# Merging the window's first block by a predicated copy in the attention maxima of a one-core transformer kernel

## The chip, the cores and the metric

The kernel runs on one core of a Trainium2 chip. The metric is the device time of one execution in microseconds (us). A core has a matrix engine (TensorE, PE in the profile, with its weight loads as PEld), a vector engine (VectorE, DVE), a scalar engine (ScalarE, ACT), GpSimd (POOL) and a sync engine (SP), which here issues the DMAs. TensorE writes its results into PSUM, a small memory of eight banks; SBUF is the larger working memory.

## The reference

One sequence of 2048 positions with 576 features passes through an attention block and an MLP-mixer block, each ahead of a residual addition and each with a layer norm that a condition vector modulates. The attention has 32 heads of width 18 and a sliding causal window: query i sees keys i-255 to i.

```python
scores = jnp.einsum("bhqd,bhkd->bhqk", q, k) * (Dh ** -0.5)
mask = (idx[:, None] - idx[None, :] >= 0) & (idx[:, None] - idx[None, :] < 256)
scores = jnp.where(mask[None, None], scores, -1e9)
p = softmax(scores, axis=-1)
o = jnp.einsum("bhqk,bhkd->bhqd", p, v)
...
h = layernorm(x) * (1 + ca) + sa
x = x + ga * (attention(h) @ wo)
h = layernorm(x) * (1 + cb) + sb
x = x + gb * mixer_block(h)
```

The softmax needs, for each query and head, a maximum over the allowed scores. Any number close to it serves for stability, but here it is the exact maximum over the window.

## The kernel before

The whole program is one hand-made schedule: every piece of work is entered with a time (`at(t, f, ...)`), the entries are sorted by time, and the instructions are issued in that order. Each engine works through its own instructions strictly in this order, and so does SP's DMA queue. The times only give an order; what really sets the pace is what each engine waits for.

The stages are the QKV projection, the attention, the output projection with two layer norms, the token mixing and the channel MLP. The change lies in the attention, which runs over 32 steps n. A step treats 512 queries (group g = n // 8) of four heads, as two pairs j of two heads. Queries and keys are cut into blocks of 64. For a query block the window touches five key blocks: the oldest, of which only the keys k > q (positions inside the block) are allowed, three full ones, and its own, of which only k <= q are allowed.

For the maxima, `mx` (L436) forms the scores of two query blocks i = 2 bb + s into one PSUM tile `pm` of two banks. There are eight such units (j, bb) in a step, and they use two PSUM tiles in turn (tags m0 and m1), so a unit can only start when the reduce of the unit two before it has read its tile. Each query block takes one matrix product of 320 columns with the keys (L444), and a second product, of the identity with a constant `Mq` (L446), which adds -1e30 to the forbidden places of the oldest and of the own block, 128 columns in all. In the first group (n < 8) query blocks 0 to 3 have fewer than five key blocks, since the sequence begins there; they mask their own block alone (L448). `red` (L450) takes the maximum: for the units with five blocks, one reduce over two times 320 columns on VectorE (L456), and for the others one reduce for each query block (L460). There are 224 units of the first kind and 32 of the second.

Once the eight units of step n are reduced, `mtr` (L464) transposes the maxima on TensorE (the instruction that the profile calls `mt`), `mev` (L468) copies them on ScalarE, and `mst` (L473) writes them by two DMAs into two rows of the query tile, so that the later score products come out with the maximum already subtracted. On SP's queue the loads of the queries and keys of a later step (L419, L421) stand behind these writes. From the loaded data POOL forms `QS` (L427), which `mx` reads, and `KS` (L434), which the later products read.

Two steps later `xm` (L480) computes the scores again, transposed and with the maxima subtracted, in ten banks a step, adding the masks with `Mk` (L489); `ex` (L504) applies the exponential on ScalarE. Every second step `av` (L526) multiplies by the values, 208 small products in a row, followed by transposes (L536) and the division by the sum on VectorE (L543, L544). On TensorE the units of `mx` are interleaved with these: one unit, one or two banks of `xm`, the next unit, and so on.

From step 12 on the output projection of one tile of 128 rows is spread over every two steps, ten tiles within the attention: transposes (L590), the split into two parts on ScalarE and VectorE (L597, L599), the products of its two halves (L611), the residual additions on VectorE (L615), and two layer norms, whose statistics (L117 to L119) and normalisation (L624, L625) are VectorE's too. The first half and the transposes fall into a step that also holds an `av` block, the second half and the norms into the next.

Of the kernel before, what the change touches and what calls it, by code (L numbers as in the profile page):

```python
# [9 lines left out]
F32R = mybir.dt.float32r  # L10
BF16 = mybir.dt.bfloat16
AF = mybir.ActivationFunctionType
ALU = mybir.AluOpType
# [6 lines left out]
P = 128  # L20
# [13 lines left out]
class Kern:  # L34
# [8 lines left out]
    def setup(self, stack):  # L43
        nc, tc = self.nc, self.tc
        self.ev = []
        self.cst = stack.enter_context(tc.tile_pool(name="cst", bufs=1))
        self.dr = stack.enter_context(tc.tile_pool(name="dr", bufs=1, space=DRAM))
        self.ps = stack.enter_context(tc.tile_pool(name="psU", bufs=1, space=PSUM))
        self.pools = {}
        c = self.cst  # L50
        self.ident = c.tile([P, P], F32, name="ident")
        self.identr = c.tile([P, P], F32R, name="identr")
        self.gb = c.tile([P, D], F32, name="gb")
        self.mhalf = c.tile([P, 1], F32, name="mhalf")
        self.rowm = c.tile([P, 8], F32, name="rowm")
        self.Mq = c.tile([P, 2, 64], F32R, name="Mq")
        self.Mk = c.tile([P, 5, 64], F32R, name="Mk")
        self.md = c.tile([P, 10], F32, name="md")
        self.qd = [self.dr.tile([2, D, 512], F32, name=f"qd{g}") for g in range(4)]
        self.kd = [self.dr.tile([2, D, 768], F32, name=f"kd{g}") for g in range(4)]  # L60
        self.vd = [self.dr.tile([P, VW], F32, name=f"vd{t}") for t in range(NT)]
        self.od = [self.dr.tile([512, D], F32, name=f"od{g}") for g in range(4)]
        self.xp = [self.dr.tile([P, D], F32, name=f"xp{t}") for t in range(NT)]
        self.hbd = [self.dr.tile([P, D], F32, name=f"hbd{t}") for t in range(NT)]
        self.xnd = [self.dr.tile([P, D], F32, name=f"xnd{t}") for t in range(NT)]
        self.modd = {v: self.dr.tile([1, D], F32, name=f"modd{v}") for v in (2, 3, 4, 5)}
# [24 lines left out]
    def masks(self):  # L91
        nc = self.nc
        g = nc.gpsimd
        for M in (self.Mq, self.Mk):
            g.memset(M.bitcast(F32), 0.0)
        h = slice(0, 64)
        sel = lambda t, s, op, cm: g.affine_select(out=t, in_=t.bitcast(F32), pattern=[[s, 64]], compare_op=op, fill=NEG, base=0, channel_multiplier=cm)
        sel(self.Mq[h, 0], 1, ALU.is_gt, -1)
        sel(self.Mq[h, 1], -1, ALU.is_ge, 1)
        sel(self.Mk[h, 0], -1, ALU.is_gt, 1)  # L100
        sel(self.Mk[h, 1], 1, ALU.is_ge, -1)
        nc.vector.tensor_copy(self.Mk[h, 3:5], self.Mk[h, 0:2].bitcast(F32))
        for M in (self.Mq, self.Mk):
            nc.vector.tensor_copy(M[64:128], M[0:64].bitcast(F32))
        m = self.rowm
        v = self.ident[:, 0:108].rearrange("p (u r d) -> p u r d", u=3, r=2)
        for r in range(2):
            nc.vector.tensor_reduce(out=m[:, r:r + 1], in_=v[:, :, r, :], axis=mybir.AxisListType.XY, op=ALU.add)
        nc.vector.tensor_tensor(out=m[:, 2:4], in0=m[:, 0:2], in1=self.ident[:, 108:110], op=ALU.add)
        nc.vector.tensor_reduce(out=m[:, 4:5], in_=self.ident[:, 108:110], axis=mybir.AxisListType.X, op=ALU.add)  # L110
# [277 lines left out]
    def attention(self, t1, t2, TA, HU, LX=2.05):  # L388
        nc, at, ps = self.nc, self.at, self.ps
# [46 lines left out]
        def mx(n, j, bb):  # L436
            g = n // 8
            pm = X["pm", n, j, bb] = ps.tile([P, 2, 512], F32, tag=f"m{bb % 2}", name=f"mx{n}_{j}_{bb}")
            Q, K = X["qs", n, j], X["K"][n % 3]
            for s in range(2):  # L440
                i = 2 * bb + s
                nb = 5 if g else min(5, i + 1)
                lhs = Q[:, i].rearrange("p r q -> p (r q)")
                nc.tensor.matmul(pm[:, s, 320 - 64 * nb:320], lhs, K[:, j, 64 * (i + 5 - nb):64 * (i + 5)], start=True, stop=False)  # L444
                if nb == 5:
                    nc.tensor.matmul(pm[:, s, 0:320].rearrange("p (a b) -> p a b", b=64)[:, 0::4, :], self.identr, self.Mq, start=False, stop=True)  # L446
                else:
                    nc.tensor.matmul(pm[:, s, 256:320], self.identr, self.Mq[:, 1], start=False, stop=True)  # L448

        def red(n, j, bb):  # L450
            if ("m", n) not in X:
                X["m", n] = a1([P, 16], F32, tag="m", name=f"m{n}", bufs=2)
            m, pm = X["m", n], X["pm", n, j, bb]
            c = 8 * j + 2 * bb
            if n >= 8 or bb >= 2:
                nc.vector.tensor_reduce(out=m[:, c:c + 2], in_=pm[:, :, 0:320], axis=mybir.AxisListType.X, op=ALU.max, negate=True)  # L456
            else:
                for s in range(2):
                    w = 64 * (2 * bb + s + 1)
                    nc.vector.tensor_reduce(out=m[:, c + s:c + s + 1], in_=pm[:, s, 320 - w:320], axis=mybir.AxisListType.X, op=ALU.max, negate=True)  # L460
# [201 lines left out]
        for n in range(N):  # L662
            at(max(t1 + .5 + n * .01, tm(n - 0.8)), load, n)
            for j in range(2):
                at(max(t1 + .6, tm(n - 0.3 + 0.5 * j)), qs, n, j)
                for bb in range(4):
                    th = n + (4 * j + bb) / 8
                    at(tm(th), mx, n, j, bb)
                    at(tm(th + .06), red, n, j, bb)
                at(max(t2 + .01, tm(n + LX - 0.5 + 0.45 * j)), ks, n, j)  # L670
                for k in range(5):
                    th = n + LX + (5 * j + k) / 10
                    at(tm(th), xm, n, j, k)
                    at(tm(th + .03), ex, n, j, k)
            at(tm(n + 1.03), mtr, n)
            at(tm(n + 1.04), mev, n)
            at(tm(n + 1.13), mst, n)
        for u in range(16):
            h = 2 * u + LX + 2
# [592 lines left out]
```

## Time and profile before

| what | before |
|---|---|
| median of 3 runs | 1869.98 us (1864.36 to 1878.24) |
| the profiled execution | 1870.27 us, span 1868.5 us |
| mean granted TensorE clock | 0.971 |
| PE busy | 1731.3 us, 93% |
| DVE busy | 1094.4 us, 59% |
| ACT busy | 707.2 us, 38% |
| POOL busy | 902.3 us, 48% |
| the units of the maxima | from 231 us to 698 us |

The busy time of a group of matrix products is the time in which at least one of them was in flight; the mean duration of one holds its latency, so neighbours overlap and the mean isn't what one product costs. A wait is told with the engine and line that released it; where several things were waited for it is the one that came last by the profile's account.

### The profile page before, as it was taken

How to read it: one execution, taken by the hardware profiler on the slowest of the kernel's cores; microseconds unless marked ns; L12 is line 12 of the kernel's file. 1: busy time of each engine (PE TensorE's matmuls, PEld its weight loads, DVE VectorE, ACT ScalarE, POOL GpSimd, SP SyncE). 2: the span in 40 equal slices, each digit the busy share in tenths (PEclk: the TensorE clock that was granted, in tenths of full speed). 3: DMA queues.
4: the chain of work that ended last, by engine and by line, in shares of the span. 5: the costliest groups of instructions: out<-in, count | busy, mean ns of one | idle time of the engine just before them, and what ended most of it. 6: DMA issues, size and time to landing. Idle time of an engine off the chain costs nothing.

```text
span 1868.5 us, 33751 instructions
## 1 busy us (share of the span) xinstructions
PE 1731.3 (93%) x13496; PEld 1579.5 (85%) x13496; DVE 1094.4 (59%) x1801; ACT 707.2 (38%) x1210; POOL 902.3 (48%) x842
## 2 busy tenths in 40 slices
PE   6999989889999997898879999999979999999998
PEld 6788878788888986797868899999978999999997
DVE  3644244455656563566667666666676666666664
ACT  2222134344444444444433333333343333333331
POOL 3312264445454442346466655555553555555560
PEclk9999979899999998899989999999989999999999
DMA  4855552444544533565352211111224222222211
GB/s 146 312 180 180 165 152 85 118 117 133 156 134 141 149 101 113 192 216 168 115 167 68 60 55 54 55 55 56 60 71 141 60 60 60 60 60 60 59 43 51
DMA packets 156132, 206.72 MB, mean 111 GB/s; under 512 B 19012, under 2 KB 87620, under 8 KB 155400
## 3 DMA queue, kind: packets, MB, share of 16 engines
q1 hardware_dynamic: 155976, 204.57, 35.8%
q8 instruction: 106, 1.74, 0.4%
q14 instruction: 50, 0.41, 0.1%
HBM read 143.69 MB, written 60.56 MB: 109 GB/s over the span
## 4 chain that ended last, share of the span: by engine, by line
PE 45%; DVE 3%; POOL 3%; DMA 2%; ACT 1%; issue 1%; SPq 1%; POOLq 0%; DVEq 0%
PE d L1128 23%; PE pg L789 1%; PE w L838 1%; DVE W L986 1%; DMA wf<-in_B_w_dram 1%; PE u18P L1075 1%; PE u19P L1075 1%; PE u29P L1075 1%; PE u33P L1075 1%; PE u32P L1075 1%; PE u31P L1075 1%; PE u30P L1075 1%; PE u28P L1075 1%; PE u27P L1075 1%; PE u26P L1075 1%
## 5 line engine op out<-in xcount | busy, mean ns | idle before, releaser
L1128 PE MATMUL d<-W,G 128*128 128x288 f32 x3456 | 505.9, 297 | 11.9 <-DVE acc L1136 9.1
L1128 PEld LDWEIGHTS d<-W,G 128*128 128x128 f32 x3456 | 487.9, 189 | 33.6 <-DVE acc L1136 10.3
L1136 DVE TENSOR_TENSOR acc<-d,acc 128x576 f32<-128x576 f32 x288 | 216.7, 753 | 195.9 <-PE d L1128 193.9
L966 POOL TENSOR_TENSOR wf<-wf 128x384 f32<-128x384 f32 x140 | 146.6, 1068 | 337.9 <-DMA wf<-in_B_w_dram 299.8
L456 DVE TENSOR_REDUCE m<-mx 128x2 f32<-128x640 f32 x224 | 181.3, 817 | 159.5 <-PE mx L446 157.3
L504 ACT ACTIVATE P<-X 128x512 f32<-128x512 f32 (+4 forms) x320 | 180.4, 573 | 207.2 <-PE X L489 204.6
L444 PE MATMUL mx<-KD,QS 128*128 128x320 f32 (+4 forms) x512 | 157.6, 358 | 38.2 <-POOL QS L427 19.4
L427 POOL TENSOR_SCALAR QS<-QD,rowm 128x512 fp32r<-128x512 f32 x128 | 87.7, 698 | 145.4 <-DMA QD<-qd 60.7
L487 PE MATMUL X<-QD,KS 128*128 128x64 f32 (+2 forms) x704 | 151.2, 307 | 3.7 <-ACT P L504 3.3
L978 POOL TENSOR_TENSOR W<-wf,W 128x768 fp32r<-128x768 f32 x70 | 151.4, 2185 | 1.2 <-ACT W L972 1.2
L1105 DVE TENSOR_TENSOR G<-U,G 128x512 fp32r<-128x512 f32 x108 | 91.0, 843 | 100.3 <-ACT G L1098 100.3
L444 PEld LDWEIGHTS mx<-KD,QS 128*128 128x128 f32 x512 | 101.9, 199 | 45.8 <-POOL QS L427 24.2
L1096 ACT ACTIVATE U<-U 128x512 f32<-128x512 f32 x108 | 68.3, 632 | 177.6 <-DVE U L1081 177.6
L1096 ACT ACTIVATE C<-C 128x512 f32<-128x512 f32 x36 | 22.8, 632 | 280.7 <-DVE C L1081 280.7
L279 PE MATMUL qk<-hT,Wqk 128*128 128x512 f32 x504 | 121.0, 401 | 0.0
L279 PEld LDWEIGHTS qk<-hT,Wqk 128*128 128x128 f32 x504 | 95.9, 191 | 24.2 <-issue 0.9
L487 PEld LDWEIGHTS X<-QD,KS 128*128 128x128 f32 x704 | 106.7, 195 | 10.6 <-ACT P L504 7.5
L434 POOL TENSOR_SCALAR KS<-KD,rowm 128x768 fp32r<-128x768 f32 (+1 forms) x128 | 107.6, 853 | 0.0
L992 POOL TENSOR_TENSOR wf<-wf,gb 128x1152 f32<-128x1152 f32 x35 | 103.5, 2956 | 6.7 <-DMA wf<-in_B_w_dram 6.7
L446 PE MATMUL mx<-Mq,identr 128*128 128x128 f32 x448 | 101.3, 226 | 0.0
L1007 POOL TENSOR_TENSOR W<-wf,W 128x1152 fp32r<-128x1152 f32 x35 | 96.7, 2762 | 6.9 <-ACT W L1001 6.9
L972 ACT CAST W<-wf 128x1152 fp32r<-128x1152 f32 x70 | 90.3, 1319 | 21.6 <-DMA wf<-in_B_w_dram 10.8
(763 smaller groups left out, 3219.5 us busy)
## 6 DMA issues: line engine op xcount, KB each, us to landing
wf<-in_B_w_dram SPq DMA_DIRECT2D x35, 576.0 KB
wf<-in_B_w_dram SPq DMA_DIRECT2D x140, 128.0 KB
KD<-kd SPq DMA_DIRECT2D x72, 216.0 KB
QD<-qd SPq DMA_DIRECT2D x96, 144.0 KB
wf<-in_B_w_dram SPq DMA_DIRECT2D x140, 64.0 KB
qd<-qs SPq DMA_DIRECT2D x16, 512.0 KB
kd<-qs SPq DMA_DIRECT2D x16, 512.0 KB
vd<-Vst SPq DMA_DIRECT2D x16, 312.0 KB
```

Source lines behind the costliest of these rows:

```text
L279: nc.tensor.matmul(po, W[:, a, fs], H[:, c, :], start=(n == 0), stop=(n == 13))
L434: nc.gpsimd.tensor_scalar(t[:, b0:, r], src[:, b0:], M[:, 2 + r:3 + r], 0.0, op0=ALU.mult, op1=ALU.add)
L444: nc.tensor.matmul(pm[:, s, 320 - 64 * nb:320], lhs, K[:, j, 64 * (i + 5 - nb):64 * (i + 5)], start=True, stop=False)
L456: nc.vector.tensor_reduce(out=m[:, c:c + 2], in_=pm[:, :, 0:320], axis=mybir.AxisListType.X, op=ALU.max, negate=True)
L487: nc.tensor.matmul(px[:, c:c + q1 - q0], K[:, b + 4].rearrange("p r k -> p (r k)"), Q[:, j, q0:q1], start=(i == 0), stop=False)
L504: nc.scalar.activation(p[:, lo:], X["px", n, j, k][:, lo:], AF.Exp, scale=SCALE)
L966: nc.gpsimd.tensor_tensor(out=WF[:, o], in0=WF[:, a], in1=WF[:, b], op=ALU.subtract)
L978: eng.tensor_tensor(out=W[:, s0:s1, 3:5, :], in0=WF[:, 1 + s0:1 + s1, 0:2], in1=W[:, s0:s1, 0:2, :].bitcast(F32), op=ALU.subtract)
L992: nc.gpsimd.tensor_tensor(out=R4, in0=R4, in1=gb.unsqueeze(1).to_broadcast([P, 2, D]), op=ALU.mult)
L1075: nc.tensor.matmul(po, W[:, w - 1, a, :], X[:, b, :], start=(m == 0), stop=(m == 6))
L1128: nc.tensor.matmul(po, G[:, g, ta, b, ts], W[:, w, b, cs], start=(n == 0), stop=(n == 5))
L1136: nc.vector.tensor_tensor(out=a, in0=po, in1=a, op=ALU.add)
```

## The change

The constant `Mq` keeps only its second half: -1e30 where k > q, 0 elsewhere. For query blocks with all five key blocks no mask product is issued any more; the product with the keys ends the accumulation. In `red`, VectorE first copies the scores of the oldest block over those of the own block wherever `Mq` isn't zero (read as integers, its -1e30 is a nonzero number), that is, wherever k > q. These are just the places that are forbidden in the own block and allowed in the oldest one. The maximum is then taken over the last four blocks, 256 columns for each query block instead of 320. Blocks at the beginning of the sequence keep the mask product of 64 columns and their reduces.

```diff
-        self.Mq = c.tile([P, 2, 64], F32R, name="Mq")
+        self.Mq = c.tile([P, 64], F32R, name="Mq")
...
-        sel(self.Mq[h, 0], 1, ALU.is_gt, -1)
-        sel(self.Mq[h, 1], -1, ALU.is_ge, 1)
+        sel(self.Mq[h], -1, ALU.is_ge, 1)
...
-                nc.tensor.matmul(pm[:, s, 320 - 64 * nb:320], lhs, K[:, j, 64 * (i + 5 - nb):64 * (i + 5)], start=True, stop=False)
-                if nb == 5:
-                    nc.tensor.matmul(pm[:, s, 0:320].rearrange("p (a b) -> p a b", b=64)[:, 0::4, :], self.identr, self.Mq, start=False, stop=True)
-                else:
-                    nc.tensor.matmul(pm[:, s, 256:320], self.identr, self.Mq[:, 1], start=False, stop=True)
+                nc.tensor.matmul(pm[:, s, 320 - 64 * nb:320], lhs, K[:, j, 64 * (i + 5 - nb):64 * (i + 5)], start=True, stop=nb == 5)
+                if nb < 5:
+                    nc.tensor.matmul(pm[:, s, 256:320], self.identr, self.Mq, start=False, stop=True)
...
             if n >= 8 or bb >= 2:
-                nc.vector.tensor_reduce(out=m[:, c:c + 2], in_=pm[:, :, 0:320], axis=mybir.AxisListType.X, op=ALU.max, negate=True)
+                late = self.Mq.bitcast(mybir.dt.int32).unsqueeze(1).to_broadcast([P, 2, 64])
+                nc.vector.copy_predicated(pm[:, :, 256:320], late, pm[:, :, 0:64])
+                nc.vector.tensor_reduce(out=m[:, c:c + 2], in_=pm[:, :, 64:320], axis=mybir.AxisListType.X, op=ALU.max, negate=True)
```

## The prediction

> **What bounds the kernel now.** I read the windows of busy time first, to find which engine each stretch of the attention hangs on, then the timelines of TensorE (PE) and VectorE (DVE) inside one step, then the waits. Columns of the windows: stretch, its length, busy us of PE, PEld, DVE, ACT and POOL with instruction counts, granted TensorE clock, DMA share, GB/s.
>
> ```profile
> 332.98:348.19 15.21, 15.05 (x214) 12.47 (x212) 7.81 (x13) 6.02 (x13) 8.06 (x13) 0.82 0.35 95
> 637.22:654.94 17.72, 17.30 (x303) 16.29 (x303) 8.97 (x16) 8.19 (x16) 9.23 (x12) 1.00 0.40 115
> 654.94:667.55 12.61, 11.11 (x82) 10.46 (x82) 9.90 (x17) 6.15 (x11) 5.07 (x10) 1.00 0.55 159
> 657.94:667.55 9.61, 8.11 (x60) 7.46 (x59) 9.22 (x16) 5.42 (x10) 5.07 (x10) 1.00 0.71 207
> ```
>
> A step is one n, from one transpose `mt` of the maxima to the next. From n = 12 on steps come in pairs. The long one (second row) holds an `av` block and the first half of an output-projection tile: PE is busy 17.30 of 17.72 us and DVE half the time, so PE sets it. The short one (third row) holds the tile's residual additions and both layer norms: in its last 9.61 us (fourth row) DVE is busy 9.22 and PE 8.11, so there DVE sets it. The first row, a long step ahead of n = 12, is PE's (15.05 of 15.21).
>
> The PE timeline of that short step (start, duration, in brackets the idle time before and what ended it):
>
> ```profile
> 654.94 0.28 PE L464 MATMUL mt<-ident,m 128*16 128x128 f32 x1 [0.42 <-DVE xr L615]
> ...
> 657.27 0.31 PE L444 MATMUL mx<-KD,QS 128*128 128x320 f32 x1
> 657.42 0.22 PE L446 MATMUL mx<-Mq,identr 128*128 128x128 f32 x1
> 657.48 0.36 PE L444 MATMUL mx<-KD,QS 128*128 128x320 f32 x1
> 657.68 0.22 PE L446 MATMUL mx<-Mq,identr 128*128 128x128 f32 x1
> 657.74 0.47 PE L487 MATMUL X<-QD,KS 128*128 128x192 f32 x2
> ...
> 666.86 0.38 PE L444 MATMUL mx<-KD,QS 128*128 128x320 f32 x1 [0.62 <-POOL c8rs L120]
> ...
> 667.55 0.28 PE L464 MATMUL mt<-ident,m 128*16 128x128 f32 x1
> ```
>
> and DVE beside it:
>
> ```profile
> 653.70 0.82 DVE L456 TENSOR_REDUCE m<-mx 128x2 f32<-128x640 f32 x1 [1.76 <-PE mx L446]
> 654.44 0.45 DVE L615 TENSOR_TENSOR xr<-wo,xr 128x288 f32<-128x288 f32 x1
> 654.80 0.81 DVE L456 TENSOR_REDUCE m<-mx 128x2 f32<-128x640 f32 x1
> 657.94 0.83 DVE L456 TENSOR_REDUCE m<-mx 128x2 f32<-128x640 f32 x1 [2.32 <-PE mx L446]
> 658.68 0.45 DVE L615 TENSOR_TENSOR xr<-wo,xr 128x288 f32<-128x288 f32 x1
> 659.04 0.45 DVE L117 BATCH_NORM_STATS2 b8st<-xr 128x6 f32<-128x288 f32 x1
> 659.41 0.45 DVE L118 BATCH_NORM_STATS2 b8st<-xr 128x6 f32<-128x288 f32 x1
> 659.89 0.21 DVE L119 BATCH_NORM_AGGREGATE b8mv<-b8st 128x2 f32<-128x12 f32 x1
> 660.02 1.50 DVE L456 TENSOR_REDUCE m<-mx 128x2 f32<-128x640 f32 x2
> 661.67 0.82 DVE L456 TENSOR_REDUCE m<-mx 128x2 f32<-128x640 f32 x1 [0.15 <-PE mx L446]
> 662.42 1.03 DVE L624 SCALAR_TENSOR_TENSOR h<-xr,b8mv,cb 128x576 f32<-128x576 f32 x1
> 663.55 0.82 DVE L625 SCALAR_TENSOR_TENSOR h<-h,b8rs,sb 128x576 f32<-128x576 f32 x1
> ```
>
> From 657.94 DVE has one gap, 0.15 us. PE's wait of 0.62 at 666.86 is put down to a small POOL instruction, but this `mx` needs the PSUM buffer that the reduce two units earlier frees, and DVE is the engine with work queued; I read it as a DVE wait. The step ends when the last reduce is done and `mt` may go. Two rows of the waits frame this:
>
> ```profile
> PE mx L444 <- POOL QS L427: 19.4, 8, 4.3
> ```
> ```profile
> PE mt L464 <- DVE xr L615: 4.2, 10, 0.4
> ```
>
> The second (total, times, longest) shows ten long steps, each ended by a wait for DVE's addition L615, which stands behind a reduce (653.70, 654.44). The first is another limit, ahead of n = 12: there the short steps are ended by loads. One of them, from SP's, POOL's and PE's timelines:
>
> ```profile
> 322.89 0.50 SPq L419 DMA_DIRECT2D QD<-qd  x1
> ```
> ```profile
> 330.55 1.36 POOL L427 TENSOR_SCALAR QS<-QD,rowm 128x512 fp32r<-128x512 f32 x2 [9.82 <-DMA KD<-kd]
> ```
> ```profile
> 331.96 0.63 PE L444 MATMUL mx<-KD,QS 128*128 128x320 f32 x1 [3.47 <-POOL QS L427]
> ```
>
> The load goes out behind the `mt` of the step before, its data and QS come 9 us later, and PE stands still for 3.47 us. PE work taken out of such a step only lengthens the wait.
>
> **The change, part by part.** A unit is two query blocks: two 320-column products, and for the units concerned two mask products and one reduce.
>
> ```profile
> L456 DVE TENSOR_REDUCE m<-mx 128x2 f32<-128x640 f32 x224 | 181.3, 817 | 159.5 <-PE mx L446 157.3
> ```
> ```profile
> L1128 PE MATMUL d<-W,G 128*128 128x288 f32 x3456 | 505.9, 297 | 11.9 <-DVE acc L1136 9.1
> ```
>
> *Mask products off PE.* 224 units lose two each, 448 in all. Their mean of 0.22 us is a latency that overlaps the next product, so I price by start to start. A unit takes 657.74 - 657.27 = 0.47 us now. Two products of 320 columns alone: a stream of 288-column products takes 505.9/3456 = 0.146 each, times 320/288 is 0.16, so 0.32 for two. The saving is 0.15 us a unit, 34 us over all 224. Its upper end: the products of a unit that comes behind a wait start more slowly (0.38 instead of 0.31 at 666.86), and with weight loads that no longer have to hide behind a short product I allow 0.25. Its lower end, 0.10, is the two mask starts alone (657.48 - 657.42 and 657.74 - 657.68, 0.06 each).
>
> *The reduce, 512 instead of 640 elements.* The form rows on DVE:
>
> ```profile
> L460 DVE TENSOR_REDUCE m<-mx 128x1 f32<-128x128 f32 x16 | 4.5, 281 | 0.0
> L600 DVE TENSOR_TENSOR T<-pb,T 128x128 fp32r<-128x128 f32 x13 | 3.7, 281 | 0.0
> L460 DVE TENSOR_REDUCE m<-mx 128x1 f32<-128x64 f32 x16 | 3.5, 220 | 14.9 <-PE mx L448 14.8
> ```
>
> 64 elements cost 61 ns, so 128 fewer save 0.12. A reduce now occupies DVE for 0.74 (657.94 to 658.68); it will for 0.62.
>
> *The predicated copy.* The trace has none. It moves 128 elements from PSUM to PSUM under a mask from SBUF. Nearest is L600, 128 elements from PSUM with a second stream from SBUF: 0.28. Low end: the 64-element reduce, 0.22, since it handles at least as many. High end: the 288-element addition L615, 0.45, if writing PSUM or the predicate costs more. Nothing below 0.22 is plausible for an instruction that streams. I take 0.28. The reduce reads what the copy writes and can't overlap it: between dependent DVE instructions lie 0.03 (659.41 + 0.45 to 659.89) to 0.10 (662.42 + 1.03 to 663.55); I take 0.06. A unit then costs DVE 0.62 + 0.28 + 0.06 = 0.96 instead of 0.74: +0.22, with ends +0.13 (0.22 and 0.03) and +0.43 (0.45 and 0.10).
>
> The next reduce starts 0.74 us behind one that lasts 0.83, so DVE instructions overlap at their ends. The Trainium skill (VectorE: DVE Perf Modes, "The DRAIN you can't avoid") says that the next op does not start until the pipeline is empty; the trace disagrees for independent instructions. By that rule the unit would go from 0.82 to about 0.98, the surcharge would be 0.16 and the total some 5 us lower than mine, an estimate.
>
> *Where it lands.* Short steps from n = 12: seven units lie between 657.94 and `mt`. DVE needs 7 x 0.22 = 1.54 more, the gap of 0.15 closes, and the first of these units arrives 0.15 earlier: +1.24 us. Queued behind each copy are that unit's reduce and the norms; PE's `mx` two units on waits for them, and `mt`, SP's write of the maxima and the next load wait for the last. Long steps: seven units ahead of the addition that `mt` waits for give 7 x 0.15 = 1.05, and the reduce ahead of that addition costs 0.22: -0.83. The eighth unit's saving goes into the wait. A pair: +0.41; ten pairs: +4.1 us. Ahead of n = 12: four steps are PE's own (n = 4, 6 with four units each, n = 8, 10 with eight): 24 x 0.15 = 3.6, less 4 x 0.22 for the reduce ahead of their `mt`: -2.7. The other steps there end with a load: nothing.
>
> *Set-up.* One mask select fewer on POOL, half of the first row; POOL then idles for 7 us, so nothing, and 0.2 us without that cover.
>
> ```profile
> 3.39 0.42 POOL L97 TENSOR_SCALAR_AFFINE_SELECT Mq<-Mq 64x64 fp32r<-64x64 f32 x2
> ...
> 11.17 0.23 POOL L120 TENSOR_SCALAR a0rs<-a0mv 128x1 f32<-128x1 f32 x1 [6.98 <-DVE a0mv L119]
> ```
>
> Sum: +4.1 - 2.7 = +1.4. The profiled execution took 1870.27 us (span 1868.5), 0.3 above the median of the three runs, so I forecast 1871 us. Low end (PE 0.25, DVE +0.13): short 0.91 - 0.15 - 0.25 = +0.51, long -1.75 + 0.13 = -1.62, ten pairs -11, early -6.0 + 0.5; 1854. High end (PE 0.15, DVE +0.43): short 3.01 - 0.30 = +2.71, long -1.05 + 0.43 = -0.62, ten pairs +21, early -3.6 + 1.7; 1889.
>
> **The rivals.** *PE's saving comes through.* For it: PE is busy over 90% of the attention, and DVE idles through every `av` block. Against: with only two PSUM buffers for the maxima DVE cannot use that idle time for the next units, and the short steps are full. Even with a free merge (surcharge 0) they keep DVE's length: -0.3, pair -1.35, total -17. Over 1% takes a saving of 0.25 as well: short -0.40, long -1.75, ten pairs -21.5, early -6: 1843. Chance 0.13.
>
> *The copy is dear and DVE becomes the bound.* It decides from a copy of 0.45 us on; at 0.6 (gap 0.06) the unit costs DVE 1.28, +0.54. Short 3.78 - 0.30 = +3.5, long at best -1.05 + 0.54 = -0.5, ten pairs +30, early -1.4: about 1899, and more once long steps wait for DVE as well. For it: no row shows DVE writing PSUM or a predicated write. Against: L600 has the same streams at 0.28. Chance 0.17.
>
> *The mask products were nearly free.* If 0.10 a unit is all that goes: short +1.29, long -0.7 + 0.22, ten pairs +8, early -1.5: 1877. Chance 0.06.
>
> **How the numbers follow.** The forecast has 0.64: PE gains in the long steps what DVE loses in the short ones. About 1%, 19 us, is what a measurement of this kernel can tell from no change. Faster is the first rival, 0.13; slower the second, 0.17; within 1% the forecast and the third, 0.70. The range of 1854 to 1889 is the span of the unknown prices and leaves out the outer parts of the first two rivals.
>
> **What would show it.** The profile after should hold 224 predicated copies near 0.28 us and reduces near 0.70; a unit of two products 0.32 us from start to start; short steps of about 13.9 us with DVE over 95% busy behind the norms and more PE waits on the maxima; long steps of about 16.9. Waits for QS ahead of n = 12 should stay or grow. I am wrong if the short steps get no longer, if the copy lasts 0.45 or more, or if the reduce starts before the copy ends.

## The result and the profile after

The changed kernel takes 1884.87 us (median of 8 runs, 1879.65 to 1892.01), the kernel before 1872.32 us (median of 8): ratio 1.0065, 95% interval [1.0046, 1.0085]. It is slower by 0.65%, inside the range and within the 1% of the forecast, but 14 us above the 1871 us that were predicted, and clear of no change. The profiled execution has a span of 1883.1 us against 1868.5, and a mean granted clock of 0.963 against 0.971. The lower clock is not that of one execution alone: all eight of the changed kernel lie at 0.959 to 0.965, those of the kernel before in the comparisons below at 0.965 to 0.974.

The two groups on VectorE that answer to the old reduce, from the page of the changed kernel (busy us and mean ns behind the first bar):

```profile
L455 DVE TENSOR_REDUCE m<-mx 128x2 f32<-128x512 f32 x224 | 154.8, 691 | 7.7
...
L454 DVE COPY_PREDICATED mx<-Mq,mx 128x128 f32<-128x128 int32 x224 | 64.6, 289 | 136.1 <-PE mx L443 133.8
```

Copy and reduce have the predicted sizes, 0.29 and 0.69 us. The timeline of VectorE at the end of a short step of the changed kernel (start, duration) shows what three units cost in a row:

```profile
674.50 0.27 DVE L454 COPY_PREDICATED mx<-Mq,mx 128x128 f32<-128x128 int32 x1
674.81 0.69 DVE L455 TENSOR_REDUCE m<-mx 128x2 f32<-128x512 f32 x1
675.42 0.28 DVE L454 COPY_PREDICATED mx<-Mq,mx 128x128 f32<-128x128 int32 x1
675.74 0.69 DVE L455 TENSOR_REDUCE m<-mx 128x2 f32<-128x512 f32 x1
676.34 0.28 DVE L454 COPY_PREDICATED mx<-Mq,mx 128x128 f32<-128x128 int32 x1
```

A unit occupies VectorE for 0.92 us (674.50 to 675.42), 0.18 more than the 0.74 before. On TensorE's timeline a unit of two products now takes 0.29 us (665.42 to 665.71) instead of 0.47, and the waits of the short step have grown:

```profile
665.42 0.45 PE L443 MATMUL mx<-KD,QS 128*128 128x320 f32 x2
665.71 0.42 PE L486 MATMUL X<-QD,KS 128*128 128x192 f32 x2
...
673.67 0.56 PE L443 MATMUL mx<-KD,QS 128*128 128x320 f32 x2 [1.06 <-DVE m L455]
...
675.71 0.53 PE L443 MATMUL mx<-KD,QS 128*128 128x320 f32 x2 [1.18 <-POOL c8rs L120]
...
676.48 0.28 PE L463 MATMUL mt<-ident,m 128*16 128x128 f32 x1 [0.25 <-DVE m L455]
```

The windows of two pairs of steps of the changed kernel (stretch, length, busy us of PE, PEld, DVE, ACT, POOL, granted clock, DMA share, GB/s), each from `mt` to `mt`, short step first, and below them the second short step from its first predicated copy on:

```profile
534.10:547.50 13.40, 9.94 (x65) 8.71 (x66) 10.99 (x26) 6.15 (x11) 5.98 (x10) 1.00 0.54 157
547.50:566.74 19.24, 17.54 (x287) 14.82 (x288) 10.05 (x24) 8.17 (x16) 8.81 (x12) 0.91 0.35 103
663.09:676.48 13.39, 9.91 (x65) 8.67 (x65) 10.99 (x26) 6.13 (x11) 5.48 (x10) 1.00 0.59 173
676.48:693.76 17.28, 16.05 (x286) 14.38 (x286) 10.04 (x24) 8.18 (x16) 8.83 (x12) 1.00 0.37 103
...
665.91:676.48 10.57, 7.09 (x45) 5.85 (x43) 10.16 (x24) 5.58 (x10) 5.48 (x10) 1.00 0.74 218
```

The pair of the kernel before that answers to the first (n = 21 and 22) is:

```profile
532.69:545.29 12.60, 11.11 (x82) 10.46 (x82) 9.89 (x17) 6.14 (x11) 5.06 (x10) 1.00 0.58 161
545.29:563.48 18.19, 17.34 (x303) 16.24 (x302) 8.96 (x16) 8.17 (x16) 9.23 (x12) 1.00 0.42 113
```

Short steps went from 12.60 to 13.40 us. From the first copy on VectorE is busy 10.16 of 10.57 us, so its queue sets them. The last long step shown is 0.4 us shorter than its counterpart before (17.70). But most long steps came out longer, like the first one: its granted clock is 0.91. Microsecond by microsecond, from the windows of the changed kernel, in the `av` block that follows the short step:

```profile
548.00:549.00 1.00, 1.00 (x18) 0.48 (x25) 0.38 (x1) 0.71 (x2) 1.00 (x2) 0.72 0.22 85
549.00:550.00 1.00, 1.00 (x50) 0.96 (x41) 0.00 (x0) 0.00 (x0) 1.00 (x2) 0.50 0.03 5
550.00:551.00 1.00, 1.00 (x56) 0.99 (x48) 0.00 (x0) 0.00 (x0) 1.00 (x3) 0.50 0.31 79
```

TensorE, busy all the time, runs at half its clock for 3.4 us (548.44 to 551.86 by the trace's record of the clock). Of the nine long steps n = 14 to 30 this happens in seven; before, in one. Added up over the whole stretch from `mt` of n = 11 to `mt` of n = 31, which grew from 309.1 to 321.1 us: the ten short steps +7.8 us, the ten long ones +4.2. Two of the long steps ran at clock 1.00 (n = 16 and 30) and were 0.43 and 0.42 us shorter than before; had all ten been so, they would have given back 4.3. So some 8.5 us of the loss go with the clock, an estimate by this difference. Ahead of the first `mt` the profile after is 1.5 us shorter. Ahead of n = 12 the stretch from the first `mt` fell by 1.1 us (144.2 to 143.1). Behind the attention the two profiles differ by 5 us, in a part that the change doesn't touch and that differs by as much between other profiles of this study (1170.6 to 1178.5 us); I count it as scatter.

### The profile page after: what moved, and what is told of

It reads as the page before. It is cut to its first block, busy times and chain, and to the rows that moved or that the text cites. A ratio compares the mean times of both kernels' runs of the same rounds, so it can differ in the third digit from the quotient of the medians.

```text
span 1883.1 us, 33137 instructions
## 1 busy us (share of the span) xinstructions
PE 1707.0 (91%) x13048; PEld 1529.1 (81%) x13048; DVE 1130.6 (60%) x2025; ACT 706.0 (37%) x1210; POOL 903.0 (48%) x841
## 4 chain that ended last, share of the span: by engine, by line
PE 43%; DVE 3%; POOL 3%; ACT 2%; issue 2%; DMA 1%; SPq 1%; POOLq 0%; DVEq 0%
PE d L1127 22%; DMA wf<-in_B_w_dram 1%; PE pg L788 1%; DVE W L985 1%; PE w L837 1%; PE u33P L1074 1%; PE u30P L1074 1%; PE u24P L1074 1%; PE u22P L1074 1%; PE u21P L1074 1%; PE u8P L1074 1%; PE u5P L1074 1%; PE u4P L1074 1%; PE u32P L1074 1%; PE u31P L1074 1%
## 5 line engine op out<-in xcount | busy, mean ns | idle before, releaser
L1127 PE MATMUL d<-W,G 128*128 128x288 f32 x3456 | 507.0, 297 | 15.5 <-DVE acc L1135 12.6
L443 PE MATMUL mx<-KD,QS 128*128 128x320 f32 (+4 forms) x512 | 133.3, 337 | 61.5 <-POOL QS L426 18.3
L455 DVE TENSOR_REDUCE m<-mx 128x2 f32<-128x512 f32 x224 | 154.8, 691 | 7.7
L1104 DVE TENSOR_TENSOR G<-U,G 128x512 fp32r<-128x512 f32 x108 | 97.5, 903 | 100.2 <-ACT G L1097 100.2
L486 PE MATMUL X<-QD,KS 128*128 128x64 f32 (+2 forms) x704 | 146.4, 300 | 6.9 <-ACT P L503 6.3
L454 DVE COPY_PREDICATED mx<-Mq,mx 128x128 f32<-128x128 int32 x224 | 64.6, 289 | 136.1 <-PE mx L443 133.8
L443 PEld LDWEIGHTS mx<-KD,QS 128*128 128x128 f32 x512 | 85.7, 200 | 74.2 <-POOL QS L426 25.4
L486 PEld LDWEIGHTS X<-QD,KS 128*128 128x128 f32 x704 | 111.2, 195 | 20.8 <-ACT P L503 17.7
```

The source lines that it names most:

```text
L455: nc.vector.tensor_reduce(out=m[:, c:c + 2], in_=pm[:, :, 64:320], axis=mybir.AxisListType.X, op=ALU.max, negate=True)
L486: nc.tensor.matmul(px[:, c:c + q1 - q0], K[:, b + 4].rearrange("p r k -> p (r k)"), Q[:, j, q0:q1], start=(i == 0), stop=False)
L1127: nc.tensor.matmul(po, G[:, g, ta, b, ts], W[:, w, b, cs], start=(n == 0), stop=(n == 5))
```

## The experiments

The theory after the result: from n = 12 on VectorE's queue sets the short steps, so the copy lengthens them; TensorE then idles more in them, and its clock is lowered in the `av` block behind; ahead of n = 12 the loads end every second step. The rival is that TensorE's own work sets the attention. What each kernel did, worked out from windows from `mt` to `mt` ("short": median of the steps n = 13 to 29; "share": PE's busy share in the 4.5 us ahead of the `mt` that ends them, mean of these nine; "drops": how many of the nine long steps n = 14 to 30 had a granted clock of 0.98 or less; "to 11" and "11 to 31": us from the first `mt` to that of n = 11, and from there to the last). All but the ratio come from one profiled execution of each kernel.

| kernel | ratio [95%] | short | share | drops | to 11 | 11 to 31 |
|---|---|---|---|---|---|---|
| before | 1 | 12.61 | 0.72 | 1 | 144.2 | 309.1 |
| changed | 1.0065 [1.0046, 1.0085] | 13.40 | 0.46 | 7 | 143.1 | 321.1 |
| copy only | 1.0126 [1.0107, 1.0144] | 13.63 | 0.60 | 5 | 146.1 | 327.8 |
| masks gone only | 0.9982 [0.9962, 1.0002] | 12.45 | 0.53 | 5 | 139.6 | 310.1 |
| merge in even steps | 0.9999 [0.9984, 1.0015] | 12.61 | 0.68 | 2 | 141.1 | 308.9 |
| changed, masks in odd steps | 1.0065 [1.0043, 1.0088] | 13.63 | 0.57 | 4 | 139.9 | 321.4 |
| changed, waits filled | 1.0052 [1.0031, 1.0073] | 13.64 | 0.62 | 3 | 142.3 | 320.7 |
| changed, late norms | 0.9969 [0.9952, 0.9987] | 12.06 | 0.52 | 9 | 142.2 | 309.0 |
| before, late norms | 0.9949 [0.9920, 0.9978] | 11.78 | 0.71 | 0 | 144.1 | 299.3 |
| late norms, merge in even steps | 0.9929 [0.9900, 0.9958] | 11.93 | 0.64 | 5 | 142.2 | 303.6 |
| changed, late norms, early load | 0.9730 [0.9708, 0.9752] | 10.13 | 0.93 | 0 | 126.0 | 279.5 |
| before, late norms, early load | 0.9782 [0.9750, 0.9814] | 10.53 | 0.99 | 0 | 126.8 | 287.6 |
| late norms, early load, merge in even steps | 0.9751 [0.9729, 0.9773] | 10.53 | 0.95 | 0 | 126.8 | 283.7 |
| changed, early load | 1.0007 [0.9985, 1.0028] | 14.16 | 0.40 | 9 | 127.6 | 334.6 |

### The two halves of the change by themselves

The copy and the shorter reduce, with the mask products kept on TensorE (what they mask, the copy overwrites or the reduce leaves out), as a change to the kernel before:

```diff
             if n >= 8 or bb >= 2:
-                nc.vector.tensor_reduce(out=m[:, c:c + 2], in_=pm[:, :, 0:320], axis=mybir.AxisListType.X, op=ALU.max, negate=True)
+                late = self.Mq[:, 1].bitcast(mybir.dt.int32).unsqueeze(1).to_broadcast([P, 2, 64])
+                nc.vector.copy_predicated(pm[:, :, 256:320], late, pm[:, :, 0:64])
+                nc.vector.tensor_reduce(out=m[:, c:c + 2], in_=pm[:, :, 64:320], axis=mybir.AxisListType.X, op=ALU.max, negate=True)
```

> VectorE part alone: the mask products stay on TensorE, the predicated copy and the reduce over 256 columns are added for every unit with five key blocks. Theory (VectorE sets the short steps from n = 12 on, 0.19 us more for each of seven units; a lower granted clock comes on top only where TensorE idles more): short steps 12.6 to about 13.6 us, long steps about +0.2, together about +13 us, ratio 1.007; the clock drops in the av blocks are rarer than in the changed kernel, since TensorE is busier. Rival (TensorE sets the attention and VectorE has room): ratio 1.000, short steps unchanged.

Measured: 1.0126, 1895.85 us. A short and a long step of it, from its windows:

```profile
640.01:653.64 13.63, 11.12 (x81) 10.48 (x81) 11.00 (x25) 6.11 (x11) 5.49 (x10) 1.00 0.60 172
686.07:705.19 19.12, 18.50 (x304) 16.82 (x302) 10.25 (x24) 8.19 (x16) 8.71 (x12) 0.94 0.33 91
```

The short step is 13.63, as expected: with TensorE's work as before (11.12), VectorE's alone makes it a microsecond longer. The rival, by which VectorE had room, falls. The total is larger than I expected. The ten long steps took 8.2 us more where 2 were forecast, since the clock drops came here too, in five of nine; the rest of the excess lies outside the steps from n = 12 on (1.9 us up to n = 11, 4.9 us behind the attention).

The other half, again as a change to the kernel before: no mask products, the reduce over all 320 columns, no copy.

```diff
-                nc.tensor.matmul(pm[:, s, 320 - 64 * nb:320], lhs, K[:, j, 64 * (i + 5 - nb):64 * (i + 5)], start=True, stop=False)
+                nc.tensor.matmul(pm[:, s, 320 - 64 * nb:320], lhs, K[:, j, 64 * (i + 5 - nb):64 * (i + 5)], start=True, stop=nb == 5)
-                if nb == 5:
-                    nc.tensor.matmul(pm[:, s, 0:320].rearrange("p (a b) -> p a b", b=64)[:, 0::4, :], self.identr, self.Mq, start=False, stop=True)
-                else:
+                if nb < 5:
                     nc.tensor.matmul(pm[:, s, 256:320], self.identr, self.Mq[:, 1], start=False, stop=True)
...
-            nc.scalar.activation(p[:, lo:], X["px", n, j, k][:, lo:], AF.Exp, scale=SCALE)
+            nc.scalar.activation(p[:, lo:], X["px", n, j, k][:, lo:], AF.Exp, scale=SCALE / 16)
```

> TensorE part alone: no mask products on units with five key blocks, the reduce over 320 columns stays, no copy. The maxima then also cover forbidden keys, and the exponential is taken of scores scaled down by 16 so that it stays finite; both are left-out parts of the computation and cost no time. Theory: short steps stay near 12.4 us, since VectorE's work in them is unchanged, long steps -1.0, ahead of n = 12 about -4: -14 us, ratio 0.992, or up to 8 us more than that where the clock drops because TensorE idles in the short steps. Rival (TensorE sets the attention): 184 units at 0.15 to 0.18 us, -28 to -33 us, ratio 0.983 to 0.985, short steps about 11.4 us.

Measured: 0.9982, nothing that can be told from no change. The rival's 0.983 to 0.985 is out, and so is the theory's 0.992; the 6 us that the theory left where the clock drops lie within the interval. Its windows, a long step at full clock and the short one behind it:

```profile
635.04:652.12 17.08, 16.06 (x286) 14.38 (x287) 8.85 (x16) 8.18 (x16) 9.29 (x12) 1.00 0.41 116
652.12:664.56 12.44, 9.79 (x66) 8.63 (x66) 10.11 (x18) 6.23 (x11) 5.07 (x10) 1.00 0.58 168
```

With 1.3 us of TensorE's work gone from it the short step is only 0.17 us shorter: it is VectorE's. Its four long steps at full clock are 0.2 to 0.6 us shorter than before (the one shown 17.08 against 17.72), and five clock drops take that back. So TensorE's saving was mostly not on the path, and where it was, the drops behind the idler short steps took it back.

### Merging only where TensorE sets the step

```diff
+        mask = lambda n: n >= 12 and n % 2 == 1
+        merge = lambda n: n < 12 or n % 2 == 0
```

(`mask` decides on the mask products of `mx`, `merge` on copy and shorter reduce; the next kernels are told by the same two.)

> The merge by copy only where TensorE sets the step: all steps ahead of n = 12 and the even steps from there on; odd steps n >= 13 keep the mask products and the reduce over 320 columns. Theory: short steps 12.6 us as before, long steps -0.4, ahead of n = 12 -2.7, granted clock in the av blocks back at 1.00: -7 us, ratio 0.996. Rival (the clock drops because of the lighter long steps or by chance): av blocks still at a lower clock, ratio 1.000 or above.

Measured: 0.9999. Short steps are at 12.61 and the drops down to two, as expected, and the stretch to n = 11 is 3 us shorter. But the nine long steps together are only 0.1 us shorter: two drops and, in some, a slower `av` block (5.64 us at n = 28 instead of 4.81, at full clock; why, no run shows) use up the gain of 0.4 us a step. The forecast of 0.996 lies outside the interval, which allows a gain of 3 us at most. The clock came out as the theory has it, the time as the rival has it.

### Giving TensorE more work in the waits

Two kernels test whether idling is what lowers the clock. The first puts the mask products back in the odd steps:

```diff
+        mask = lambda n: n >= 12 and n % 2 == 1
+        merge = lambda n: True
```

> The changed kernel, with the mask products put back on TensorE in the odd steps n >= 13 only, where they are not needed (the copy overwrites what they would mask): TensorE does more work in the steps in which it waits for VectorE anyway. Theory (the clock is lowered because TensorE idles too much in the short steps): the av blocks run at clock 1.00 again, short steps about 13.5 us, long steps about -0.4 against before: +3 us against before, ratio 1.001, about 10 us faster than the changed kernel with more work. Rival (the clock drops have another cause, or the loss is all waits): no faster than the changed kernel, ratio 1.007 or above.

Measured: 1.0065, as the changed kernel; the gain of 10 us did not come. The drops fell from seven to four, not to none, and the short steps grew to 13.63 us, since the first unit of the step reaches VectorE 0.17 us later (3.00 us behind `mt` instead of 2.83). The second adds more, at another place:

```diff
-            nc.tensor.matmul(o, self.identr, mv, start=False, stop=True)
+            extra = 2 if n >= 11 and n % 2 == 1 else 0
+            for e in range(extra + 1):
+                nc.tensor.matmul(o, self.identr, mv, start=False, stop=e == extra)
```

> The changed kernel, and in the short steps from n = 13 on each of the ten mask products of the transposed scores is issued three times instead of once (what is masked is exp(-huge) = 0 either way): some 2.6 us of TensorE work in steps in which TensorE waits 3.4 us of 13.4. Theory (the granted clock falls in the av blocks because TensorE idles too much in the short step before): short steps 13.4 to 13.8 us, clock 1.00 in nearly all long steps, these 17.3 to 17.8 us: faster than the changed kernel by about 5 us, ratio against before about 1.004. Rival (the drops have nothing to do with idling): as many drops, and the added work makes it slower than the changed kernel, ratio 1.008 or more.

Measured: 1.0052. Windows of a short and a long step:

```profile
661.43:675.07 13.64, 11.70 (x85) 11.01 (x86) 11.01 (x26) 6.25 (x11) 5.49 (x10) 1.00 0.58 168
675.07:692.35 17.28, 16.05 (x287) 14.34 (x288) 10.05 (x24) 8.18 (x16) 8.81 (x12) 1.00 0.36 103
```

Twenty more products a step leave it as fast as the changed kernel. Drops fell from seven to three and the nine long steps by 2.6 us (167.35 to 164.72), while the short steps lost 0.24 us each. Four drops less would have given more, but four of the six long steps at full clock hold an `av` block of 5.15 to 5.62 us instead of 4.81; what slowed it no run shows. That the drops follow TensorE's idling is borne out by the direction of both kernels and by the "share" column: kernels with 0.40 to 0.53 have five to nine drops of nine, with 0.57 to 0.64 three to five, with 0.68 to 0.72 none to two, and with 0.93 or more none. That work put into the waits pays is not: I expected 5 us from it and got none that can be measured.

The traces' records of the clock tell more than the share. In all fourteen the clock changes only on a grid of 3.413 us. Windows of the changed kernel cut on this grid, two at the end of the short step n = 19 and two at the end of n = 29 (columns as above):

```profile
510.90:514.31 3.41, 1.48 (x10) 1.14 (x9) 3.31 (x8) 1.54 (x3) 1.92 (x4) 1.00 0.64 211
514.31:517.72 3.41, 3.09 (x38) 1.97 (x39) 1.99 (x5) 0.85 (x2) 3.31 (x6) 0.50 0.32 97
671.32:674.74 3.42, 2.14 (x14) 1.65 (x13) 3.25 (x8) 1.76 (x4) 1.36 (x2) 1.00 0.62 182
674.74:678.15 3.41, 2.20 (x52) 1.60 (x59) 2.51 (x6) 1.27 (x3) 3.22 (x6) 1.00 0.50 172
```

Step n = 19 has the higher share over its last 4.5 us (0.50 against 0.45), but its waits fall into one window, in which TensorE is busy for 43%, and the next window is halved; in n = 29 they are split between two windows (63% and 64%), and the clock stays. In the fourteen traces together, from `mt` of n = 11 to that of n = 31, a window at full clock in which TensorE was busy for less than 58% was followed by a halved one in all 43 cases, from 58% to 64% in 8 of 22, and above that in none of 1107. That idling within one such window takes the clock away is shown by this as well as by the kernels above; which of two equally idle steps is hit depends on where the grid cuts them. In the two kernels with filled waits, windows of 48% to 62% are left ahead of their seven drops.

### Taking VectorE's other work out of the short steps

The layer norms of the ten tiles are entered later, so that on VectorE they stand behind the step's last reduce and run in the `av` block, in which VectorE idled:

```diff
-            at(tm(h + 0.90), ln1, t)
-            at(tm(h + 1.0), st1, t)
-            at(tm(h + 1.25), ln1n, t)
-            at(tm(h + 1.40), ln2, t)
-            at(tm(h + 1.5), st2, t)
-            at(tm(h + 1.80), ln2n, t)
-            at(tm(h + 1.95), st3, t)
+            e = (1.56, 1.565, 1.57, 1.58, 1.85, 1.90, 2.05) if t < 10 else (0.90, 1.0, 1.25, 1.40, 1.5, 1.80, 1.95)
+            for d, f in zip(e, (ln1, st1, ln1n, ln2, st2, ln2n, st3)):
+                at(tm(h + d), f, t)
```

On the changed kernel:

> The changed kernel with the layer norms of the ten tiles (statistics and normalisation, 3.8 us of VectorE each) entered so late that on VectorE they come behind the last reduce of the short step, into the av block, in which VectorE idles for 5 us. Theory (VectorE's queue sets the short steps): they fall from 13.4 us to 11.5 to 11.8, where the loads of the next queries and keys end them (QS is ready some 11.1 us after mt); long steps as in the changed kernel; TensorE is busy for 85% of the short steps, so fewer clock drops: -12 to -15 us against before, ratio 0.992 to 0.994. Rival (VectorE isn't what holds them): short steps still 13.4 us, ratio 1.0065.

On the kernel before:

> The kernel before with the same later norms. Theory: short steps fall from 12.6 us to about 11.8, with TensorE (11.1 us of work) and the loads close together; long steps unchanged, clock 1.00: -8 us, ratio 0.9955, so that with the norms out of the way the change is worth about -5 us instead of costing 12. Rival (TensorE set the short steps before): 12.6 us, ratio 1.000.

Measured: 0.9969 and 0.9949, the second as forecast, the first short of its 0.992 to 0.994. Short steps fell to 12.06 and 11.78 us: VectorE's queue had set them in both kernels, most of all in the changed one (13.40). But with the norms away the changed kernel is still no faster than the one before. Its TensorE waits 1.8 to 2.5 us in one piece in each short step, here from its timeline, with POOL's:

```profile
571.72 0.76 PE L447 MATMUL mx<-KD,QS 128*128 128x320 f32 x2 [1.78 <-DVE b5mv L119]
```
```profile
570.30 1.36 POOL L427 TENSOR_SCALAR QS<-QD,rowm 128x512 fp32r<-128x512 f32 x2 [10.22 <-DMA QD<-qd]
```

(the name in the first line's brackets is again only what came last; `QS`, formed from the loaded queries, is ready at 571.66 us), and all nine long steps have a drop, against none in the other; fewer drops were forecast. Merging only in the even steps, with late norms:

> Later norms, and the merge only in the steps ahead of n = 12 and in the even steps from there on (odd ones keep the mask products). Theory: short steps and granted clock as with the later norms on the kernel before (11.8 us, no drops), long steps 0.4 shorter: -4 us beside that kernel, ratio against before 0.992 to 0.993. Rival (the merge costs clock wherever it is used): ratio 0.995 or above.

Measured: 0.9929, not separable from the 0.9949 without any merge. Five drops came back, which the theory did not expect; its share is 0.64.

### Loads ahead of the maxima on SP's queue

```diff
-            at(max(t1 + .5 + n * .01, tm(n - 0.8)), load, n)
+            at(max(t1 + .5 + n * .01, tm(n - 0.95)), load, n)
```

The load of the next queries and keys now stands ahead of the two writes of the maxima instead of behind them. With the late norms, on the changed kernel, on the kernel before, and with the merge in even steps:

> The changed kernel with the later norms, and with the load of the next queries and keys entered ahead of the write of the maxima on SP's queue instead of behind it, which issues it some 1.9 us earlier. Theory (with the norms out of the way the loads end the short steps, and the wait for them lowers the clock): short steps from 11.8 to 10.4 to 10.8 us, TensorE busy for about 90% of them, few clock drops; the short steps ahead of n = 12 lose 1 to 2 us of their wait too: ratio 0.980 to 0.985. Rival (loads aren't the limit): as without the earlier load, 0.997.

> The kernel before (mask products everywhere, no merge) with the later norms and the earlier load. Theory: short steps from 11.8 to about 11.2 us, TensorE's own length; ahead of n = 12 the short steps shrink by 1 to 2 us: ratio 0.985 to 0.988. With both other limits gone the mask products then cost what TensorE pays for them, and this kernel is slower than the merged one with the same two edits, by 10 to 15 us. Rival (VectorE's surcharge still counts): the two are equal or this one is faster.

> Later norms, earlier load, merge ahead of n = 12 and in even steps only. Theory: short steps as with mask products everywhere (about 11.2 us), long steps 0.4 shorter, ahead of n = 12 as in the merged kernel: between the other two, ratio 0.982 to 0.986.

Measured: 0.9730, 0.9782 and 0.9751, 1826.0, 1832.0 and 1829.4 us, each about 0.7% below its forecast. A short and a long step of the fastest one:

```profile
585.89:596.01 10.12, 9.65 (x66) 8.62 (x66) 7.81 (x18) 6.14 (x11) 4.31 (x6) 1.00 0.69 200
596.01:613.45 17.44, 15.92 (x287) 14.46 (x287) 13.54 (x32) 8.29 (x16) 10.65 (x16) 1.00 0.42 120
```

TensorE is busy 9.65 of 10.12 us in the short step, no long step drops, and the part up to n = 11 is 17 us shorter than in the changed kernel. This is the kernel that beats both, by 2.7% against the one before. Now the change pays: with both edits the merged kernel takes 279.5 us from n = 11 on and the one with mask products 287.6. The medians differ by 6 us; I expected 10 to 15, and the two intervals just touch. It is still far from the 29 us that 160 units at 0.18 us take off TensorE (an estimate): in the long step n = 30, for one, TensorE waits 0.67 us for `QS` and 0.84 us for the addition ahead of `mt`, against 0.16 and 0.42 us in the kernel with mask products.

The earlier load alone, on the changed kernel:

> The changed kernel with the earlier load alone; the norms stay where they are. Theory (from n = 12 on VectorE's queue sets the short steps, so an earlier load frees nothing there, and TensorE idles and loses clock as before; ahead of n = 12 the loads end the short steps): the part up to mt of n = 11 shrinks by 15 to 17 us as in the two kernels with both edits, short steps from n = 12 on 13.4 us with the same clock drops: -4 us against before, ratio 0.998. Rival (the loads were the limit throughout, and the later norms added little): ratio 0.975 to 0.980.

Measured: 1.0007. Up to n = 11 it gains 15.5 us like the others, and from n = 12 on it gives 13.5 back: all nine long steps drop, and the short steps n = 13 to 21 are slowed as well (14.2 us, at a granted clock of 0.94 to 0.96). I had expected 13.4 us and the same drops as in the changed kernel. So neither edit alone does it: with the norms in VectorE's way an earlier load leaves TensorE idler still at the end of the short steps (a share of 0.40 against 0.46).

## Why the prediction was right, and where it was off

**What it rested on held.** TensorE gains in the long steps what VectorE loses in the short ones: short steps at full VectorE, and a wait on the maxima and on `mt`. VectorE's half alone costs 1.26%; TensorE's half alone shortens the long steps at full clock, though its gain in the whole can't be told from none. The price of the copy, which no row before showed, was taken from L600 at 0.28 and is 0.289 us on average (271 to 297 ns); neither the dear copy nor the free merge came. The rule on the pipeline that the prediction sets beside this price is not at odds with the trace: the same paragraph of the Trainium skill (VectorE: DVE Perf Modes, "The DRAIN you can't avoid") adds that a next op that is not held starts earlier, as the addition does that starts 0.74 us after a reduce of 0.83 us (658.68 and 657.94).

That the time fell within the range is luck as far as the clock goes: the upper end of 1889 us was worked out from a copy of 0.45 us, and the loss came from elsewhere.

**Short steps: +0.8 instead of +1.24 us.** The unit's surcharge was 0.18 instead of 0.22, mostly since the reduce starts 0.03 us after the copy ends and not 0.06. And the first normalisation instruction of the norms, 1.02 to 1.03 us in all ten tiles before, lasts 0.81 in all ten of the changed kernel; why, no run shows.

**Long steps at full clock: -0.43 instead of -0.83 us.** The step that failed is "seven units ahead of the addition that `mt` waits for give 7 x 0.15". A unit by itself gave more, 0.18, but few of the seven are on the path. The last two stand beside a chain that does not shrink: transposes, split on ScalarE and VectorE, products, addition. Of the five ahead of it the first and the last, with what follows each, gave 0.23 us and the three between them nothing, since TensorE then waits for ScalarE, for `P` and for the copies `avs` ahead of `ot`; so the stretch from `mt` to `pa` shrank from 11.73 to 11.27 us. TensorE's timeline before:

```profile
648.95 0.60 PE L590 MATMUL pa<-ident,or 128*128 128x128 f32 x4
...
651.06 2.13 PE L611 MATMUL wo<-Wo,T 128*128 128x288 f32 x14
```

and after:

```profile
684.76 0.50 PE L486 MATMUL X<-QD,KS 128*128 128x256 f32 x2 [0.20 <-ACT P L503]
...
687.75 0.60 PE L589 MATMUL pa<-ident,or 128*128 128x128 f32 x4
...
689.86 2.13 PE L610 MATMUL wo<-Wo,T 128*128 128x288 f32 x14
693.76 0.28 PE L463 MATMUL mt<-ident,m 128*16 128x128 f32 x1 [0.84 <-DVE xr L614]
```

From `pa` to `wo` it is 2.11 us in both, from `wo` to `mt` 3.88 and 3.90. I had found the wait at the end of this chain, but not the one in its middle, which this row of the waits before shows:

```profile
PE wo L611 <- DVE T L599: 5.3, 9, 1.3
```

A pair at full clock thus cost +0.79 - 0.43 = +0.36 us where +0.41 was forecast: both terms were too large by 0.4, and it is by luck that their errors cancelled.

**The clock.** This is the term that the sum lacked, some 8.5 of the 12 us in the profiles. Every wait was priced at its own length. That idling 3.5 of 13.4 us, in pieces of about 1 us, would also slow the `av` block behind it was in no rival.

**Ahead of n = 12: -1.1 instead of -2.7 us.** Here the granted clock moves from run to run with the long waits for loads (n = 4 took 12.74 us at clock 1.00 before and 15.27 at 0.81 after), so that a term of this size can't be read from one profile. The waits of TensorE for `QS`, which were to stay or grow, are 18.3 us in total after 19.4. Whether anything is gained where loads end a step stays open for the same reason.

## What to carry to other kernels

An engine at 60% over the whole run can be full in the one stretch that sets the pace; moving work onto it is to be priced there, and the same work may cost nothing once what fills that stretch, and the limit behind it (here the loads), is out of the way. Removing work from the busiest engine pays only in steps that it ends itself: here the merge cost 0.65% while VectorE and the loads ended the short steps, and was worth 6 us once both were out of the way. And a wait of TensorE may cost more than its length, so look at the granted clock of the block behind it, and at how much of each 3.4 us TensorE is busy ahead of it.

## What the runs showed of the hardware

The clock of TensorE was halved for 3.4 us at a time without any long idle stretch: the longest wait in the short steps n = 13 to 29 of the changed kernel is 1.21 us, and yet seven of nine long steps dropped. In the fourteen traces the clock changes on a grid of 3.413 us, and from n = 11 on what decided was TensorE's busy share of the window before: under 58% always a drop (43 cases), 58% to 64% sometimes (8 of 22), above that never (1107). Out of a halved window the clock came back when TensorE had been busy for over 90% of it (61 cases), and stayed halved when not (11). The shares are those of this program's products as the profile accounts them. The Trainium skill (TensorE: Matmul & The Clock Gate, "What's actually happening") puts the throttled state behind an idle window of about 3.4 us, watched by a free-running window; the half rate, the length of the drop and the grid agree with that, the need for a whole idle window does not. The Trainium skill's section "A second HAM failure mode: psum-queue depth-cycling" on the same page tells of a kernel in which short idles between groups of products are enough, and the runs here agree with that.

A predicated copy on VectorE of 128 fp32 elements from PSUM to PSUM, its int32 mask in SBUF, takes 0.289 us on average, about as much as an ordinary two-stream instruction of that size (0.281), and a reduce that reads what it wrote starts 0.03 us after its end (34 to 35 ns in all 224).
